# Values of the first four pieces loaded in fp32 by SyncE's queue, with the first steps of a retention and hard-swish kernel put in another order

## The chip, the cores and the metric

The kernel runs on one core of one Trainium2 chip. The metric is the device time of one execution in microseconds (us), lower is better; the median of several runs is given. A core has five engines with a program of their own: TensorE (PE, matrix products), VectorE (DVE), ScalarE (ACT), GpSimd (POOL) and SyncE (SP). Transfers are issued by an engine and carried out by 16 DMA engines. In this kernel POOL issues the loads that change fp32 to fp16 on the way (the profile's queue q0, "software_dynamic"), SP issues plain transfers and transposes (queue q1, "hardware_dynamic").

## What is computed

```python
def _attn_ref(q, k, v):                       # 8 batches, 8 heads, 576 positions, 64 wide
    scores = scale * np.matmul(q, k.transpose(0, 1, 3, 2))
    gamma = 1.0 - 2.0 ** (-5.0 - np.arange(H))
    Dmat = np.where(rel >= 0, gamma[:, None, None] ** rel, 0.0)   # rel = row - column
    return np.matmul(scores * Dmat[None], v)

def _moe_ref(x, w_in, w_out):                 # 4608 tokens, 512 wide, 2048 hidden
    h = x @ w_in
    g = h * np.clip(h + 3.0, 0.0, 6.0) / 6.0
    return g @ w_out
```

The first part is attention with a decay in place of the softmax, so it can be worked off in pieces of 128 positions with a state carried from piece to piece. Its output, 4608 tokens of 512, goes through a two-layer network with a hard swish between the layers.

## The kernel before

**Tiling.** The sequences are cut into pieces of 128 positions of one batch, all 8 heads at once (`pieces`, lines 55 to 61). The first four pieces, 0 to 3, are the first 128 positions of batches 0 to 3; pieces 4 to 7 the next 128 positions of the same batches, and so on. Four pieces make a block of 512 tokens (`xt`), and a block is the unit of the network: `w_in` (G1, lines 438 and 461, 16 chunks `fc` of 128 hidden units), the activation (445 on ACT, 446 on DVE), `w_out` (G2, line 488, or the seven-product form at line 547 from the second block on).

**One piece.** Its keys are turned by PE (`k_by_pe`, line 296) and copied by ACT into the tile `qk`; its queries are turned and scaled by PE (`q_by_pe`, line 304; for pieces 0 to 3, which `EARLY = 4` names, against the tile `d2`, line 315) and copied by ACT (line 320). Then come the scores (`scores`, line 346, eight matmuls into one tile `sc`; for piece 3 `scores_two`, line 656, into two banks), the causal mask on DVE (line 350, or 664 for piece 3, with half of it first copied to `raw` by ACT, line 660), the scaled values `vs` on DVE (`scale_v`, line 288), the output `o` by PE (line 378), and its copy into `xt` by ACT (line 261, for piece 3 half by DVE). `update_mm` (line 402) forms the product of keys and values `u`, `update_state` (line 416) scales it by `gc` into the state `ts` on DVE. `spread_state` copies `ts` later into a block-diagonal tile that the pieces of the next round read.

**Order.** The order on each engine is written out by hand (`manual_schedule`). Every engine works its own list in order; a wait at one instruction holds all behind it on that engine. The stretch that the change touches is the start, up to the first full-width G1 matmul (line 438). PE's order there, with `warm` standing for matmuls on zeros of 512 columns: 8 warm; keys 0; 1 warm; queries 0; 2 warm; scores 0; keys 1; 2 warm; queries 1; 3 warm; scores 1; output 0; `u` 0; keys 2; 2 warm; queries 2; output 1; `u` 1; 1 warm; keys 3; scores 2; queries 3; 3 warm; scores 3; output 2; G1 chunks 0 and 1 for the first 256 tokens (line 461); output 3; `u` of 2 and 3; G1 chunks 0 and 1 for the other 256 tokens; then G1 chunks 2 to 15 at full width (line 438).

**Loads.** POOL's list of loads, in order: queries 0; keys 1, queries 1, values 1; keys 2, queries 2; keys 3, queries 3; values 2; 256 columns of `w_in`; values 3; the rest of `w_in` in five loads; half of `w_out`; piece 4; the other half of `w_out`; and so on. All of them change fp32 to fp16 on the way. SP's list begins with two plain fp32 loads of 256 KB, keys 0 and values 0 (`whole`, line 138). ACT casts keys 0 to fp16 (line 192); values 0 go into `scale_v` as fp32.

**Constants.** DVE makes the identity, `d2` (line 183), `dq` (line 188, used from piece 4 on), eight small fills of `lgc` and four fills of the block-diagonal tiles (line 208) before the first mask; ACT makes `gc` (lines 200 and 201) before it copies the turned keys of piece 0 (line 302).

Of the kernel before, what the change touches and what calls it, by code (L numbers as in the profile page):

```python
# [10 lines left out]
FP32 = mybir.dt.float32  # L11
FP16 = mybir.dt.float16
# [5 lines left out]
def kernel(  # L18
# [78 lines left out]
    def by_twos(b, s0):  # L97

        return q[b, :, s0:s0 + P, :].rearrange("h (g t) d -> g h (t d)", t=2)

    def q2_tile(c):

        tag, bufs = (("part1", 1), ("part5", 1), ("part6", 1), ("osb2", 3))[c]
        return work.tile([HALF, H, 2 * D], FP16, tag=tag, bufs=bufs, name=f"q2_{c}")

    def load(c, parts="kqv"):
        if c not in loaded:
            kn = nat.tile([P, H, D], FP16, tag="kn", bufs=NBUF, name=f"kn_{c}")
            qv = nat.tile([P, 2, H, D], FP16, tag="qv", bufs=NBUF, name=f"qv_{c}")
            loaded[c] = {"kn": kn, "qv": qv, "q16": qv[:, 0]}  # L110
            if c < EARLY:
                loaded[c]["q2"] = q2_tile(c)
        to = {"k": (loaded[c]["kn"], k), "q": (loaded[c]["qv"][:, 0], q),
              "v": (loaded[c]["qv"][:, 1], v)}
        for dst, src in (to[part] for part in parts):
            for p0, b, s0, n in pieces[c][3]:
                if src is q and c < EARLY:
                    nc.gpsimd.dma_start(loaded[c]["q2"], by_twos(b, s0))
                    continue
                nc.gpsimd.dma_start(dst[p0:p0 + n],  # L120
                                    src[b, :, s0:s0 + n, :].rearrange("h s d -> s h d"))

# [5 lines left out]
    def load_wout(c0, c1):  # L128
# [6 lines left out]
    wide = const.tile([P, P + 1], FP32)  # L135
    nc.gpsimd.iota(wide, pattern=[[1, P + 1]], base=-1, channel_multiplier=-1,
                   allow_small_or_imprecise_dtypes=True)
    def whole(src, c):

        x = work.tile([P, DM], FP32, tag="osb", bufs=4, name=f"whole_{src.tensor.name}_{c}")  # L140
        x = x.rearrange("s (h d) -> s h d", h=H)
        nc.sync.dma_start(x, src[0, :, c * P:c * P + P, :].rearrange("h s d -> s h d"))
        return x

    k0, v0 = whole(k, 0), whole(v, 0)
    loaded[0] = {"kn": nat.tile([P, H, D], FP16, tag="kn", bufs=NBUF, name="kn_0"),
                 "q2": q2_tile(0), "v": v0}
    nc.gpsimd.dma_start(loaded[0]["q2"], by_twos(0, 0))
    zeros = const.tile([P, MBLK], FP16)
    nc.vector.memset(zeros, 0.0)  # L150
    cb = const.tile([P, 2], FP32)
# [10 lines left out]
    for t in range(2):  # L162
# [21 lines left out]
        out=d2, in0=ident16[0:HALF, None, 0:HALF].to_broadcast([HALF, 2 * H, HALF]),  # L184
        in1=g2q.rearrange("g t h -> g (t h)")[:, :, None].to_broadcast([HALF, 2 * H, HALF]),
        op=ALU.mult)
    dq = const.tile([P, H, P], FP16)
    nc.vector.tensor_tensor(out=dq, in0=ident16[:, None, :].to_broadcast([P, H, P]),
                            in1=gq[:, :, None].to_broadcast([P, H, P]), op=ALU.mult)
    gqv = const.tile([P, 2, H, D], FP16)  # L190
    nc.scalar.copy(gqv[:, 1], gv[:, :, None].to_broadcast([P, H, D]))
    nc.scalar.copy(loaded[0]["kn"], k0)
    lgc = const.tile([P, NPAIR], FP32)
    for p in range(NPAIR):
        nc.vector.memset(lgc[0:HALF, p:p + 1], lng[2 * p])
# [1 line left out]


    gc = const.tile([P, 2, NPAIR], FP32)
    nc.scalar.activation(gc[:, 0], lgc, ACTF.Exp, scale=float(P))  # L200
    nc.scalar.activation(gc[:, 1], lgc, ACTF.Exp, scale=float(HALF))

    def fill_gq():
        nc.scalar.copy(gqv[:, 0], gq[:, :, None].to_broadcast([P, H, D]))
# [1 line left out]
    spare = [const.tile([P, NPAIR, P], FP16, name=f"tbd{i}") for i in range(GROUP)]  # L206
    for bd in spare:
        nc.vector.memset(bd, 0.0)

    warmed = [0]  # L210

    def warm(n, cols):

        if n == 0:
            return
        w = psum.tile([P, MBLK], FP32, tag="ph", bufs=4, name=f"warm_{warmed[0]}")
        warmed[0] += 1
        for _ in range(n):
            nc.tensor.matmul(w[:, 0:cols], zeros[:, 0:P], zeros[:, 0:cols],
                             start=True, stop=True)  # L220

    warm(8, MBLK)

    mask_rest = const.tile([P, P], FP16)

# [56 lines left out]
    def scale_v(c, parts=1):  # L282
        vs = work.tile([P, 2, H, D], FP16, tag="vs", bufs=6, name=f"vs_{c}")
        st.setdefault(c, {})["vs"] = vs[:, 1]
        v16 = loaded[c]["v"] if "v" in loaded[c] else loaded[c]["qv"][:, 1]
        for i in range(parts):
            r = slice(i * H // parts, (i + 1) * H // parts)
            nc.vector.tensor_tensor(out=vs[:, 1, r], in0=v16[:, r], in1=gqv[:, 1, r],
                                    op=ALU.mult)
# [14 lines left out]
    def q_by_pe(c, tag="ph"):  # L304
        qk = qk_of(c)
        pq = psum.tile([P, NPAIR, P], FP32, tag=tag, bufs=4 if tag == "ph" else 1,
                       name=f"trq_{c}")
        if c < EARLY:
            q2 = loaded[c]["q2"]
            pq = pq.rearrange("x p (t g) -> x p t g", t=2)  # L310
            for p in range(NPAIR):
                for t in range(2):
                    for h2 in range(2):
                        h = 2 * p + h2
                        nc.tensor.matmul(pq[h2 * HALF:h2 * HALF + HALF, p, t],
                                         q2[:, h, t * D:t * D + D], d2[:, t * H + h],
                                         start=(p == 0 and t == 0),
                                         stop=(p == NPAIR - 1 and t == 1),
                                         skip_group_check=True)
            nc.scalar.copy(qk[:, 0].rearrange("x p (g t) -> x p t g", t=2), pq)  # L320
            return
        q16 = loaded[c]["q16"]
        for p in range(NPAIR):
            for h2 in range(2):
                r = slice(h2 * HALF, h2 * HALF + HALF)
                nc.tensor.matmul(pq[r, p, :], q16[:, 2 * p + h2, :], dq[:, 2 * p + h2, :],
                                 start=(p == 0), stop=(p == NPAIR - 1), skip_group_check=True)
        nc.scalar.copy(qk[:, 0], pq)
# [61 lines left out]
    def update_mm(cs):  # L390

        cs = [c for c in cs if pieces[c][0] != "rest"]
        if not cs:
            return
        u = psum.tile([P, len(cs), NPAIR, D], FP32, tag="tu", name=f"u_{cs[0]}")
        for j, c in enumerate(cs):
            kn, vs = loaded[c]["kn"], st[c]["vs"]
            st[c]["u"] = u[:, j]
            for p in range(NPAIR):
                for h2 in range(2):  # L400
                    r = slice(h2 * HALF, h2 * HALF + HALF)
                    nc.tensor.matmul(u[r, j, p, :], kn[:, 2 * p + h2, :], vs[:, 2 * p + h2, :],  # L402
                                     start=(j == 0 and p == 0),
                                     stop=(j == len(cs) - 1 and p == NPAIR - 1),
                                     skip_group_check=True)

    def update_state(c):
        kind, b, i, _ = pieces[c]
        if kind == "rest":
            return  # L410
        u = st[c]["u"]
        scale = gc_b[1 if i == PER - 1 and b % 2 else 0]
        tag, bufs = ("tf", B) if i == PER - 1 else ("ts", 2 * GROUP)
        ts = work.tile([P, NPAIR, D], FP16, tag=tag, bufs=bufs, name=f"ts_{c}")
        if i == 0:
            nc.vector.tensor_tensor(out=ts, in0=u, in1=scale, op=ALU.mult)
        else:
            ta = work.tile([P, NPAIR, D], FP32, tag="ta", bufs=2, name=f"ta_{c}")
            nc.vector.tensor_tensor(out=ta, in0=u, in1=state_of[b], op=ALU.add)
            nc.vector.tensor_tensor(out=ts, in0=ta, in1=scale, op=ALU.mult)  # L420
        state_of[b] = ts

    def spread_state(c, copy=nc.scalar.copy):

# [196 lines left out]


    WQ = DFF // 4
    load(1)
    load(2, "kq")
    load(3, "kq")
    load(2, "v")
    load_win(0, WQ // 2)
    load(3, "v")
    for f0, f1 in ((1, 2), (2, 3), (3, 4), (4, 6), (6, 8)):  # L630
        load_win(f0 * WQ // 2, f1 * WQ // 2)
    for i in range(4):
# [4 lines left out]
    def output(c, *tags):  # L637
        inter(c, *tags)
        intra(c)

    def masked(c, filled=0):
        warm(filled, MBLK)
        scores(c, 0)
        run_later(9)
# [24 lines left out]
    k_by_pe(0)  # L669
    warm(1, MBLK)  # L670
    q_by_pe(0)
    warm(2, MBLK)
    masked(0)
    scale_v(0)
    scale_v(1)
    k_by_pe(1)
    warm(2, MBLK)
    q_by_pe(1)
    masked(1, 3)
    output(0)  # L680
    update_mm([0])
    update_state(0)
    k_by_pe(2)
    warm(2, MBLK)
    q_by_pe(2)
    output(1)
    update_mm([1])
    update_state(1)
    warm(1, MBLK)
    k_by_pe(3)  # L690
    masked(2)
    q_by_pe(3)
    scale_v(2)
    warm(3, MBLK)
    mask_two = scores_two(3)
    mask_two()
    scale_v(3, 2)
    output(2)
    for c in range(5, 8):
        load(c)  # L700
    next_load = [8]
# [212 lines left out]
    done, last = slice(0, 3 * P), slice(3 * P, MBLK)  # L914
    for fc in range(2):
        g1_columns(0, fc, banks[fc], slice(0, 2 * P))
    output(3, "o", "sc")
    update_mm([2, 3])
    update_state(2)
# [71 lines left out]
```

## Time and profile before

| what | value |
|---|---|
| median of 3 runs | 292.28 us (292.03 to 293.57) |
| the profiled execution, its own time | 292.02 us |
| its span, first to last instruction | 290.2 us |
| busy in the span: PE / DVE / ACT / POOL | 283.2 / 236.5 / 181.5 / 107.0 us |
| mean granted TensorE clock | 0.997 |

Busy time by stretch of the span (us):

| stretch | PE | DVE | ACT | POOL | moved, GB/s |
|---|---|---|---|---|---|
| 0 to 7 | 5.15 | 5.38 | 4.31 | 6.09 | 140 |
| 7 to 10 | 2.64 | 2.14 | 1.69 | 3.00 | 161 |
| 10 to 15 | 4.87 | 3.82 | 3.72 | 5.00 | 178 |
| 15 to 20 | 4.96 | 4.06 | 3.49 | 3.85 | 202 |
| 20 to 25 | 5.00 | 4.41 | 3.95 | 1.35 | 206 |
| 25 to 30 | 5.00 | 4.88 | 4.34 | 1.66 | 185 |
| 30 to 40 | 10.00 | 4.13 | 2.20 | 6.35 | 181 |

PE's busy time before the full-width G1 contains the matmuls on zeros, which compute nothing: a busy PE is no progress there. Progress is read from the chain of waits, and from when the first full-width G1 matmul begins.

### The profile page before, as it was taken

The page shows a single profiled execution, that of the slowest core. Times are in us where ns is not written, and L with a number is a line of the kernel's source. Part 1 is how long each engine was busy: PE and PEld are TensorE (multiplying, and loading weights), DVE is VectorE, ACT ScalarE, POOL GpSimd, SP SyncE. Part 2 cuts the span into 40 slices and gives each one's busy share as a digit, 9 for nine tenths or more (in the row PEclk, how much of TensorE's full clock was granted, in tenths as well). Part 3 has the DMA queues.
Part 4 walks back from the last instruction along what each step waited for, and adds up shares of the span by engine and source line. Part 5 has one row for each costly group of instructions (what it writes and reads, how often), then busy time and mean ns, then how long its engine had stood idle before and what let it go on. Part 6 is the DMA issues. An engine that isn't in the chain of part 4 may idle for free.

```text
span 290.2 us, 6739 instructions
## 1 busy us (share of the span) xinstructions
PE 283.2 (98%) x2702; PEld 185.3 (64%) x2702; DVE 236.5 (81%) x409; ACT 181.5 (63%) x312; POOL 107.0 (37%) x134
## 2 busy tenths in 40 slices
PE   7999999999999999999999999999999999999993
PEld 2554455548854885478547864787468746874582
DVE  7789559899979986998699869995999599818951
ACT  6678336785578567834785668665876586437711
POOL 8953678610870077007700770067455000000000
PEclk9999999999999999999999999999999999999998
DMA  9999999999999399919992999199999550021014
GB/s 141 171 203 198 192 156 216 172 150 107 105 215 158 70 97 218 150 36 100 212 152 50 88 215 169 23 90 201 174 73 97 114 127 0 2 84 64 1 38 110
DMA packets 151808, 35.84 MB, mean 123 GB/s; under 512 B 141536, under 2 KB 147680, under 8 KB 151776
## 3 DMA queue, kind: packets, MB, share of 16 engines
q0 software_dynamic: 113664, 18.10, 88.3%
q1 hardware_dynamic: 37808, 17.05, 29.1%
q8 instruction: 21, 0.34, 0.5%
q10 hardware_dynamic: 304, 0.26, 0.3%
q14 instruction: 11, 0.09, 0.1%
HBM read 36.70 MB, written 9.44 MB: 159 GB/s over the span
## 4 chain that ended last, share of the span: by engine, by line
PE 94%; DMA 2%; ACT 1%; DVE 1%; ACTq 0%; issue 0%; POOL 0%; POOLq 0%
PE ph L438 41%; PE b L547 19%; PE c L547 10%; PE pout L488 5%; PE a L547 5%; PE o L378 4%; PE sc L346 2%; PE o L267 2%; PE ph L461 2%; DMA q<-in_q_dram 2%; PE u L402 1%; PE sc L766 1%; PE trk L301 1%; ACT qk L320 1%; ACTq L478 0%; PE o L273 0%
## 5 line engine op out<-in xcount | busy, mean ns | idle before, releaser
L445 ACT ACTIVATE u<-ph,cb 128x512 f32<-128x512 f32 x144 | 98.5, 689 | 25.4 <-PE ph L438 23.3
L446 DVE SCALAR_TENSOR_TENSOR gt<-u,ph 128x512 f16<-128x512 f32 x144 | 95.8, 685 | 20.9 <-ACT u L445 18.5
L438 PE MATMUL ph<-xt,win 128*128 128x512 f16 x488 | 106.6, 379 | 0.0
L438 PEld LDWEIGHTS <-win 128*128 128x128 f16 x552 | 54.0, 98 | 63.2
L120 POOL DMA_DIRECT2D kn<-in_k_dram x39 | 33.4, 860 | 91.1 <-PE u L402 77.0
L547 PEld LDWEIGHTS <-s 128*128 128x128 f16 x512 | 49.4, 98 | 6.6 <-DVE s L521 0.2
L547 PEld LDWEIGHTS <-gt 128*128 128x128 f16 x384 | 36.3, 98 | 7.4 <-DVE gt L446 1.1
L120 POOL DMA_DIRECT2D qv<-in_v_dram x39 | 34.0, 880 | 4.1 <-DMA kn<-in_k_dram 1.9
L120 POOL DMA_DIRECT2D qv<-in_q_dram x36 | 30.9, 864 | 6.5 <-DMA wout<-in_moe_w_out_dram 3.4
L547 PE MATMUL b<-tw,s 128*128 128x256 f16 x256 | 30.6, 273 | 0.0
L350 DVE TENSOR_TENSOR at<-sc,mask_wide 128x1024 f16<-128x1024 f32 x19 | 23.2, 1223 | 8.4 <-PE sc L346 8.4
L261 ACT CAST xt<-o 128x512 f16<-128x512 f32 (+1 forms) x32 | 17.2, 576 | 19.2 <-PE o L378 17.2
L521 DVE TENSOR_TENSOR s<-gt 128x512 f16<-128x512 f16 (+1 forms) x37 | 22.7, 614 | 0.1
L557 ACT COPY part<-b 128x512 f32<-128x512 f32 x14 | 8.2, 586 | 20.1 <-PE b L547 20.1
L336 DVE TENSOR_TENSOR vs<-qv,gqv 128x1024 f16<-128x1024 f16 x28 | 19.2, 686 | 0.0
L547 PE MATMUL b<-wout,gt 128*128 128x256 f16 x128 | 15.6, 273 | 0.0
L547 PE MATMUL b<-tw,gt 128*128 128x256 f16 x128 | 15.3, 273 | 0.0
L547 PE MATMUL c<-tw,s 128*128 128x256 f16 x128 | 15.3, 273 | 0.0
L547 PE MATMUL a<-wout,gt 128*128 128x256 f16 x128 | 15.3, 273 | 0.0
L547 PE MATMUL c<-wout,s 128*128 128x256 f16 x128 | 15.3, 273 | 0.0
L772 ACT CAST raw<-sc 128x512 f16<-128x512 f32 x28 | 15.1, 592 | 0.0
L488 PE MATMUL pout<-wout,gt 128*128 128x512 f16 x64 | 14.8, 379 | 0.0
(96 smaller groups left out, 276.1 us busy)
## 6 DMA issues: line engine op xcount, KB each, us to landing
kn<-in_k_dram POOLq DMA_DIRECT2D x31, 128.0 KB, 5.8
qv<-in_v_dram POOLq DMA_DIRECT2D x31, 128.0 KB, 6.1
qv<-in_q_dram POOLq DMA_DIRECT2D x28, 128.0 KB, 6.5
out_dram<-olo SPq DMA_DIRECT2D x7, 512.0 KB, 4.4
out_dram<-ohi SPq DMA_DIRECT2D x7, 512.0 KB, 4.8
wout<-in_moe_w_out_dram POOLq DMA_DIRECT2D x4, 512.0 KB, 14.6
win<-in_moe_w_in_dram POOLq DMA_DIRECT2D x4, 256.0 KB, 6.4
win<-in_moe_w_in_dram POOLq DMA_DIRECT2D x2, 512.0 KB, 10.0
```

Source lines behind the costliest of these rows:

```text
L120: nc.gpsimd.dma_start(dst[p0:p0 + n], src[b, :, s0:s0 + n, :].rearrange("h s d -> s h d"))
L261: engines[i](xt[:, i * self.n:(i + 1) * self.n, g0:g0 + P], bank)
L336: nc.vector.tensor_tensor(out=vs, in0=loaded[c]["qv"], in1=gqv, op=ALU.mult)
L350: mask = lambda: nc.vector.tensor_tensor(out=at.rearrange("t a b s -> t (a b) s"), in0=sc.rearrange("t a b s -> t (a b) s"), in1=mask_b[pi ...
L378: nc.tensor.matmul(o.pair(p, r), vs[:, 2 * p + h2, :], at[:, h2, p, :], start=(st[c]["first"] and o.begins(p)), stop=(o.ends(p) and not mo ...
L438: nc.tensor.matmul(ph, win16[:, dmc, P * fc:P * fc + P], xt_of(kb)[:, dmc, :], start=(dmc == 0), stop=(dmc == NCC - 1))
L445: nc.scalar.activation(u, ph, ACTF.Relu, bias=cb[:, 0:1], scale=1.0 / 6.0)
L446: nc.vector.scalar_tensor_tensor(out=gts[kb][:, fc, :], in0=u, scalar=1.0, in1=ph, op0=ALU.min, op1=ALU.mult)
L488: nc.tensor.matmul(pout, gt[:, fc, P * mc:P * mc + P], wout16[:, fc, :], start=(fc == 0), stop=(fc == NFC - 1))
L521: nc.vector.tensor_tensor(out=sm[i][:, q], in0=one, in1=other, op=op)
L547: nc.tensor.matmul(my[chain][tt], left[:, k, P * tt:P * tt + P], right[:, k, :], start=(first and (tt == 0 or apart) and k == 0), stop=(k ...
L772: nc.scalar.copy(raw[:, h2], banks[h2])
```

## The change

It touches the start alone. Values 0 to 3 are all loaded by SP as fp32, 256 KB each, into tiles of their own; the first of them goes into the tile `raw` that keys 0 have been cast out of, so its issue waits for that cast, and the three others are issued behind it. POOL no longer loads values 1, 2 and 3, and its loads behind them move up. The tiles `qv` of pieces 0 to 3 are gone. `scale_v` for pieces 1 to 3 reads fp32 in place of fp16.

On PE the matmuls on zeros go from 22 to 16, and the order becomes: 7 warm; keys 0; 1 warm; queries 0; 3 warm; scores 0; keys 1; 2 warm; queries 1; 3 warm; scores 1; keys 2; queries 2; output 0; keys 3; scores 2; queries 3; output 1; `u` of 0 and 1 into one bank; scores 3; G1 chunks 0 and 1 for the first 256 tokens; output 2; output 3; `u` of 2 and 3; G1 chunks 0 and 1 for the other 256; then G1 at full width as before.

The states of pieces 0 and 1 are made by ACT in four multiplications (`first_states`), each over both pieces and one pair of heads, between ACT's copy to `raw` and its copy of output 2; DVE's two multiplications for them go. On DVE `dq` moves behind the fills of the block-diagonal tiles, and values 1 are scaled behind mask 1 instead of ahead of it. ACT makes `gc` after its copies of the turned keys and queries of piece 0 instead of before them. ACT's copy of the queries of pieces 0 to 3 writes in order and reads in strides, where it read in order and wrote in strides.

```diff
     def load(c, parts="kqv"):
-        if c not in loaded:
...
+        if "kn" not in loaded.setdefault(c, {}):
+            loaded[c].update({"kn": nat.tile([P, H, D], FP16, tag="kn", bufs=NBUF, name=f"kn_{c}")})
             if c < EARLY:
                 loaded[c]["q2"] = q2_tile(c)
+            else:
+                qv = nat.tile([P, 2, H, D], FP16, tag="qv", bufs=NBUF, name=f"qv_{c}")
+                loaded[c].update(qv=qv, q16=qv[:, 0])
...
-    def whole(src, c):
+    def whole(src, c, tag="osb", bufs=4):
...
-        nc.sync.dma_start(x, src[0, :, c * P:c * P + P, :].rearrange("h s d -> s h d"))
+        _, b, s0, n = pieces[c][3][0]
+        nc.sync.dma_start(x, src[b, :, s0:s0 + n, :].rearrange("h s d -> s h d"))
         return x
-    k0, v0 = whole(k, 0), whole(v, 0)
+    k0 = whole(k, 0, "raw", 1)
...
     nc.scalar.copy(loaded[0]["kn"], k0)
+    for c in range(EARLY):
+        loaded.setdefault(c, {})["v"] = whole(v, c, *(() if c else ("raw", 1)))
...
-    warm(8, MBLK)
+    warm(7, MBLK)
...
-            nc.scalar.copy(qk[:, 0].rearrange("x p (g t) -> x p t g", t=2), pq)
+            nc.scalar.copy(qk[:, 0].rearrange("x p (g t) -> x p g t", t=2),
+                           pq.rearrange("x p t g -> x p g t"))
...
+    def first_states(cs):
+        ts = work.tile([P, len(cs), NPAIR, D], FP16, tag="ts2", bufs=1, name=f"ts_{cs[0]}")
+        u = st[cs[0]]["u_all"]
+        for p in range(NPAIR):
+            nc.scalar.mul(ts[:, :, p, :], u[:, :, p, :], gc[:, 0, p:p + 1])
+        for j, c in enumerate(cs):
+            state_of[pieces[c][1]] = ts[:, j]
...
-    load(1)
-    load(2, "kq")
-    load(3, "kq")
-    load(2, "v")
+    for c in range(1, EARLY):
+        load(c, "kq")
     load_win(0, WQ // 2)
-    load(3, "v")
...
     q_by_pe(0)
-    warm(2, MBLK)
+    warm(3, MBLK)
     masked(0)
     scale_v(0)
-    scale_v(1)
+    fill_gc()
     k_by_pe(1)
     warm(2, MBLK)
     q_by_pe(1)
     masked(1, 3)
+    scale_v(1)
+    k_by_pe(2)
+    q_by_pe(2)
     output(0)
-    update_mm([0])
-    update_state(0)
-    k_by_pe(2)
-    warm(2, MBLK)
-    q_by_pe(2)
-    output(1)
-    update_mm([1])
-    update_state(1)
-    warm(1, MBLK)
     k_by_pe(3)
     masked(2)
     q_by_pe(3)
+    output(1)
     scale_v(2)
-    warm(3, MBLK)
+    update_mm([0, 1])
     mask_two = scores_two(3)
     mask_two()
     scale_v(3, 2)
-    output(2)
+    first_states([0, 1])
...
     for fc in range(2):
         g1_columns(0, fc, banks[fc], slice(0, 2 * P))
+    output(2)
     output(3, "o", "sc")
     update_mm([2, 3])
```

More of the change, by code (lines that the diff above doesn't have):

```diff
@@ L106, in load @@
     def load(c, parts="kqv"):
-        if c not in loaded:
-            kn = nat.tile([P, H, D], FP16, tag="kn", bufs=NBUF, name=f"kn_{c}")
-            qv = nat.tile([P, 2, H, D], FP16, tag="qv", bufs=NBUF, name=f"qv_{c}")
-            loaded[c] = {"kn": kn, "qv": qv, "q16": qv[:, 0]}
+        if "kn" not in loaded.setdefault(c, {}):
+            loaded[c].update({"kn": nat.tile([P, H, D], FP16, tag="kn", bufs=NBUF, name=f"kn_{c}")})
             if c < EARLY:
                 loaded[c]["q2"] = q2_tile(c)
-        to = {"k": (loaded[c]["kn"], k), "q": (loaded[c]["qv"][:, 0], q),
-              "v": (loaded[c]["qv"][:, 1], v)}
-        for dst, src in (to[part] for part in parts):
+            else:
+                qv = nat.tile([P, 2, H, D], FP16, tag="qv", bufs=NBUF, name=f"qv_{c}")
+                loaded[c].update(qv=qv, q16=qv[:, 0])
+        for part in parts:
+            src = {"k": k, "q": q, "v": v}[part]
             for p0, b, s0, n in pieces[c][3]:
-                if src is q and c < EARLY:
+                if part == "q" and c < EARLY:
                     nc.gpsimd.dma_start(loaded[c]["q2"], by_twos(b, s0))
                     continue
+                dst = loaded[c]["kn"] if part == "k" else loaded[c]["qv"][:, "qv".index(part)]
                 nc.gpsimd.dma_start(dst[p0:p0 + n],
@@ L137 @@
                    allow_small_or_imprecise_dtypes=True)
-    def whole(src, c):
-        x = work.tile([P, DM], FP32, tag="osb", bufs=4, name=f"whole_{src.tensor.name}_{c}")
+    def whole(src, c, tag="osb", bufs=4):
+        x = work.tile([P, DM], FP32, tag=tag, bufs=bufs, name=f"whole_{src.tensor.name}_{c}")
         x = x.rearrange("s (h d) -> s h d", h=H)
-        nc.sync.dma_start(x, src[0, :, c * P:c * P + P, :].rearrange("h s d -> s h d"))
+        _, b, s0, n = pieces[c][3][0]
+        nc.sync.dma_start(x, src[b, :, s0:s0 + n, :].rearrange("h s d -> s h d"))
         return x
-    k0, v0 = whole(k, 0), whole(v, 0)
+    k0 = whole(k, 0, "raw", 1)
     loaded[0] = {"kn": nat.tile([P, H, D], FP16, tag="kn", bufs=NBUF, name="kn_0"),
-                 "q2": q2_tile(0), "v": v0}
-    nc.gpsimd.dma_start(loaded[0]["q2"], by_twos(0, 0))
+                 "q2": q2_tile(0)}
+    load(0, "q")
     zeros = const.tile([P, MBLK], FP16)
@@ L186 @@
         op=ALU.mult)
-    dq = const.tile([P, H, P], FP16)
-    nc.vector.tensor_tensor(out=dq, in0=ident16[:, None, :].to_broadcast([P, H, P]),
-                            in1=gq[:, :, None].to_broadcast([P, H, P]), op=ALU.mult)
     gqv = const.tile([P, 2, H, D], FP16)
@@ L199, with fill_gc @@
     gc = const.tile([P, 2, NPAIR], FP32)
-    nc.scalar.activation(gc[:, 0], lgc, ACTF.Exp, scale=float(P))
-    nc.scalar.activation(gc[:, 1], lgc, ACTF.Exp, scale=float(HALF))
+    def fill_gc():
+        nc.scalar.activation(gc[:, 0], lgc, ACTF.Exp, scale=float(P))
+        nc.scalar.activation(gc[:, 1], lgc, ACTF.Exp, scale=float(HALF))
     def fill_gq():
@@ L208 @@
         nc.vector.memset(bd, 0.0)
+    dq = const.tile([P, H, P], FP16)
+    nc.vector.tensor_tensor(out=dq, in0=ident16[:, None, :].to_broadcast([P, H, P]),
+                            in1=gq[:, :, None].to_broadcast([P, H, P]), op=ALU.mult)
     warmed = [0]
@@ L395, in update_mm @@
         u = psum.tile([P, len(cs), NPAIR, D], FP32, tag="tu", name=f"u_{cs[0]}")
+        st[cs[0]]["u_all"] = u
         for j, c in enumerate(cs):
```

## The prediction, made before the result

> **What bounds the kernel now.** I read the chain of waits first, then its pieces in the first 20 us in order of time, then the timeline, then the DMA queues in short stretches. On the whole span the page says of the chain:
>
> ```profile
> PE 94%; DMA 2%; ACT 1%; DVE 1%; ACTq 0%; issue 0%; POOL 0%; POOLq 0%
> ```
>
> PE sets the end. From the first full-width G1 matmul on, the change alters no instruction, and PE is 100% busy from 20 to 60 us, so what the change is worth is how far that first matmul moves. The chain up to it (start, duration, what):
>
> ```profile
> 1.35 4.76 DMA q<-in_q_dram
> ...
> 6.16 0.46 PE trq L315 x16
> ...
> 13.16 1.23 DVE at L350
> 14.39 0.34 DVE vs L288
> ...
> 16.87 1.04 PE ph L461 x8
> 17.91 2.16 PE ph L438 x10
> ```
>
> Full-width G1 begins at 17.91. Ahead of it stand queries 0, landing at 6.11, then a ladder of PE, ACT and DVE steps; the last rungs are the masks and scalings of pieces 2 and 3 on DVE. Now the rows that I price with (timeline, then one landing of the DMA issues, us after the issue):
>
> ```profile
> 3.90 0.62 ACT L192 CAST kn<-whole_in_k_dram 128x512 f16<-128x512 f32 x1 [0.56 <-DMA whole_in_k_dram<-in_k_dram]
> ...
> 7.03 0.74 POOL L118 DMA_DIRECT2D q<-in_q_dram  x1
> ...
> 7.86 1.23 DVE L350 TENSOR_TENSOR at<-sc,mask_wide 128x1024 f16<-128x1024 f32 x1 [1.00 <-PE sc L346]
> ...
> 15.73 0.49 DVE L288 TENSOR_TENSOR vs<-qv,gqv 128x256 f16<-128x256 f16 x2
> ```
>
> ```profile
> q<-in_q_dram POOLq DMA_DIRECT2D x1, 128.0 KB, 5.4
> ```
>
> Queries 3 land at 7.03 + 5.4 = 12.43, and PE turns them at 13.05, only 0.6 later: the loads are close behind the ladder. Between queries 0 (6.11) and queries 3 seven loads of POOL land, 0.90 us apart. The DMA engines are busy throughout (nines in every slice from 4 us on), so this is a full queue. What a second queue does to it, from the queue rows (packets, MB, share) of 2 to 4, 40 to 44, 45 to 47 and 62 to 64 us in turn:
>
> ```profile
> q1 hardware_dynamic: 1898, 0.48, 108.2%
> ```
>
> ```profile
> q0 software_dynamic: 4842, 0.61, 239.7%
> ```
>
> ```profile
> q0 software_dynamic: 1230, 0.16, 123.5%
> q1 hardware_dynamic: 206, 0.38, 52.3%
> ```
>
> ```profile
> q0 software_dynamic: 1082, 0.14, 104.8%
> q1 hardware_dynamic: 736, 0.17, 69.0%
> ```
>
> SP's fp32 loads of keys 0 and values 0 ran alone at 0.24 MB/us, so 0.26 MB takes 1.05 us. POOL's queue alone makes 4842 / 4 = 1210 packets per us; beside SP's stores 615, beside SP's transposes 541. What SP's queue moves, POOL's queue loses.
>
> **The change part by part.** *Queries 0.* Before, POOL's queue had only 19 packets moved by 4.0 us, 2.6 us after its first issue, while values 0 were still moving. A load that POOL issues at 74.43 into an idle queue has its first packets in the slice at 76.0, 1.6 us after. Without values 0 in front, queries 0 land between 6.11 (nothing gained) and 5.2 (0.9 earlier). I take 5.5, nearer to the idle-queue row.
>
> *Queries 3 without SP's values.* Values 1 leave the queue ahead of them, so six loads stand between: 5.5 + 6 x 0.90 = 10.9.
>
> *SP's four values.* The first waits for the cast of keys 0, which ends at 4.52; the other three stand behind it on SP, at about 0.55 us each by SP's row for values 0, and nothing else waits on SP that early. Keys 0 took 3.1 us from issue to landing, of which 1.05 are their own bytes, and values 0 landed 1.1 after their last packets, so the first packets come 3.1 - 1.05 - 0.9 = 1.2 after the issue: 5.75. By then POOL's queue stands at what would land at 5.75 + 1.1 = 6.85, 1.35 us of work past queries 0, and 5.4 - 1.35 = 4.05 us are left before queries 3. SP's four loads are 4 x 1.05 = 4.2 us of the same engines. If the two halve them, both end together and queries 3 land 4.05 later, at 14.95. The price is not shown for this very pair. Bounds: nothing (SP's loads free beside POOL's); by the stores, 0.98 us of POOL's queue lost for 0.38 MB, so 2.7 for 1.05 MB; by the transposes POOL's queue keeps 0.45 of its rate, so 4.05 / 0.45 = 9.0 us for what is left, 0.9 more than at a half. I take the half: SP's own loads have just these 256 B rows, and the stores too left POOL's queue a half (615 of 1210).
>
> The Trainium skill says the same in "DMA: Bandwidth & Descriptors", section "Issuing engines are not separate DMA queues": whichever engine starts them, transfers run on the same 16 DMA engines and interleave, and starting them on several saves only issue time. By that rule the sum is the one made here, and without it the first rival's; the 615 of 1210 packets agree.
>
> How the engines are shared hardly matters: if SP's values come first, queries 3 are as late; if POOL's loads come first, values 0 land after 11 instead of at 8.7, and DVE, in order, holds mask 1 and all behind it.
>
> *From queries 3 to G1.* Before: 13.05 to 17.91, 4.86 us. After, the same rungs: turn, copy, scores, two masks, scaling, output 3, half copy, 8 matmuls. Scaling from fp32 costs 0.68 (row of values 0, 9.00) for 0.49: +0.19. The copy of queries took 0.74 with strided writes; a plain one of that size takes 0.59; I take 0.65, bounds 0.59 and 0.80: -0.09. ACT's four state products: copies of 512 and 256 columns cost 0.59 and 0.37, so about 0.26 for 128, 1.04 together, between `raw` and the copy of output 2. They run while DVE finishes mask 3 and scales (0.43 + 0.68), which covers them; 0.05, at most 0.3. So 5.0. The 16 G1 matmuls of 256 tokens now stand before output 2, and their `w_in`, right behind queries 3 in the queue, is there in time (1.3 us of queue, while turn, copy and scores take 1.5).
>
> *At no cost:* `dq` behind the fills (same sum, DVE still free at 6.86, a mask not due before 7); six warm matmuls fewer (PE waits for loads there); `gc` later; two state products off DVE (0.41 + 0.43), which DVE would spend waiting for scores 2.
>
> *Sum.* PE takes queries 3 at 15.0 instead of 13.05, +1.95; the path +0.15; G1 at 20.0 instead of 17.91: +2.1 us. Later loads arrive about 1 us later at most, less than G1's own shift, so nothing gives it back or adds. The profiled execution, 290.2 us of span in 292.02, becomes 294.1; the median is 0.26 above it: **294.4 us**.
>
> **The rivals.** *A, faster: SP's loads cost POOL's queue little.* Then DVE sets the pace. It is free at 6.86, where it idled 1.00 us before mask 0; from there 3 x 1.23 + 4 x 0.68 + 0.69 + 0.43 = 7.53 us back to back end scaling 3 at 14.39 instead of 16.22: -1.83, **290.5**. It decides if SP's values delay queries 3 by less than 0.55 us (10.9 to the 11.45 at which they are due). For it: both queues together moved 0.54 MB in 2 us at 45, against 0.31 for POOL's alone. Against it: POOL's packets halved there.
>
> *B, about the same: the stores' price.* Queries 3 land 2.7 late, 13.6: +0.6 on PE, +0.15 on the path: **293.0**. Against it: packets of 256 B move fewer bytes per us than the stores'.
>
> *C, much slower: the transposes' price and a cold PE.* Queries 3 land at 15.85, +0.9 over the main case. PE then waits some 3 us between output 0 and keys 3 with no matmuls on zeros left to fill it. The first eight of those took 3.60 us, 0.43 each; later two take 0.43. If that half rate returns, a few us of matmuls double; I price it at 0.8: **296.1**. "TensorE: Matmul & The Clock Gate" of the Trainium skill, section "What's actually happening", puts the return to half rate after an idle window of about 3.4 us; the trace shows only the half rate at the start.
>
> **Numbers.** What this kernel's measurement can tell from no change is about 0.5%, 1.46 us. Main case 0.43 (own range 293.5 to 295.5), A 0.31, B 0.14, C 0.12. Slower is the main case, less a thin edge, and C: 0.54; same is B and that edge: 0.15; faster A: 0.31. The range takes in A to C, 290.0 to 296.2.
>
> **What would show it.** Queue q0 near 600 packets per us between 6 and 14 us, with q1 beside it: the main case; near 1200: A. Queries 3 landing near 15, not near 11. PE idle before keys 3. Mask 0 starting near 7. Full-width G1 at 20.0; at 16.1 A holds, at 18.6 B. I am wrong if POOL's queue keeps its rate, or if queries 0 land before 5.

## The result and the profile after

The changed kernel takes 301.8 us (median of 6 runs, 301.23 to 304.24) against 292.89 us for the kernel before on the same chip: a ratio of 1.032, with a 95% interval of 1.028 to 1.037. It is slower, as forecast, but by 8.9 us and not by 2.1, and outside the range. The profiled execution took 301.43 us, with a span of 299.4 us (before: 290.2) and a mean granted clock of 0.977.

First the page of the kernel after: the engines' shares in the chain that ended last, and the granted clock in 40 slices of 7.5 us.

```profile
PEclk9956999999999999999999999999999999999999
...
PE 90%; DMA 6%; SPq 2%; ACT 0%; ACTq 0%; DVE 0%; issue 0%
```

PE's share fell from 94 to 90%; DMA and SP's issues now have 8%, where DMA had 2%. Slices 3 and 4 (15 to 30 us) run at half and six tenths of full speed. Where the DMA stands in the chain shows in its pieces in order of time, up to the first full-width G1 (line 455 now; start, duration, what):

```profile
5.45 3.74 SPq L144
...
9.24 14.50 DMA whole_in_v_dram<-in_v_dram
23.74 0.02 issue
23.76 0.44 DVE vs L294
...
24.25 0.76 PE o L385 x6
...
25.43 1.82 PE ph L478 x8
27.25 0.90 PE ph L455 x4
```

Values 3, issued by SP at 9.24, land at 23.74. Everything waits for them: DVE scales them at 23.76, PE forms output 3, the last eight G1 matmuls of 256 tokens, and full-width G1 begins at 27.25. Before, it began at 17.91. That is 9.3 us, and the two spans differ by 9.2: the whole loss lies ahead of this matmul. (In the timeline it begins some 0.2 us earlier than in the chain, at 27.04 here and at 17.75 before; where a run below shows a timeline, it is compared with these.) The scaling of values 3 began at 15.73 before, so 8.0 of it is the late landing; the other 1.3 is that the stretch from the scaling to G1 took 3.49 us instead of 2.18, nearly all of it the clock's: the last eight G1 matmuls of 256 tokens took 1.82 us where they had taken 1.04. The first row below is the wait behind it (waits of the first 28 us: total, times, longest), the next three the stretches 10 to 15, 15 to 20 and 20 to 25 us (busy time of each engine with its instructions, then granted clock, DMA share, GB/s):

```profile
DVE vs L294 <- DMA whole_in_v_dram<-in_v_dram: 8.9, 4, 3.0
```

```profile
10.00:15.00 5.00, 1.55 (x32) 1.13 (x32) 2.49 (x3) 1.66 (x3) 1.56 (x3) 0.86 1.61 188
15.00:20.00 5.00, 4.87 (x67) 3.19 (x65) 1.73 (x3) 3.37 (x8) 2.28 (x3) 0.50 1.35 185
20.00:25.00 5.00, 1.39 (x24) 1.00 (x26) 1.92 (x5) 0.88 (x2) 2.50 (x3) 0.50 1.26 200
```

DVE waited at each of the four scalings. PE was busy 1.55 of 5 us between 10 and 15, and then worked at half rate. Why SP's loads took so long shows in the queue rows of 7 to 9, 15 to 17 and 20 to 22 us in turn (packets, MB, share):

```profile
q0 software_dynamic: 722, 0.11, 73.3%
q1 hardware_dynamic: 862, 0.22, 70.1%
...
q0 software_dynamic: 491, 0.24, 87.6%
q1 hardware_dynamic: 492, 0.13, 47.0%
...
q0 software_dynamic: 376, 0.29, 90.2%
q1 hardware_dynamic: 377, 0.10, 36.0%
```

From about 14 us on, POOL's queue carries `w_in` in packets of 0.24 MB / 491 = 490 bytes and more, and SP's queue moves as many packets as POOL's, one for one. But its packets are of 256 B, so it moves 0.06 MB per us, a quarter of the 0.24 it made alone. At that pace the half megabyte of values 2 and 3 takes 8 us. (The first two rows, from 7 to 9 us, are not one for one: there POOL's queue carries keys and queries in packets of about 150 bytes.)

### The profile page after: what moved, and what is told of

The parts are those of the page before. It is cut to its first block, busy times and chain, and to the rows that moved or that the text cites. A ratio compares the mean times of both kernels' runs of the same rounds, so it can differ in the third digit from the quotient of the medians.

```text
span 299.4 us, 6732 instructions
## 1 busy us (share of the span) xinstructions
PE 286.4 (96%) x2696; PEld 186.8 (62%) x2696; DVE 237.2 (79%) x407; ACT 182.3 (61%) x316; POOL 104.4 (35%) x131
## 4 chain that ended last, share of the span: by engine, by line
PE 90%; DMA 6%; SPq 2%; ACT 0%; ACTq 0%; DVE 0%; issue 0%
PE ph L455 40%; PE b L564 19%; PE c L564 10%; DMA whole_in_v_dram<-in_v_dram 5%; PE pout L505 5%; PE a L564 5%; PE o L385 3%; PE sc L353 2%; PE o L273 2%; PE ph L478 2%; SPq L144 2%; PE u L410 1%; PE sc L775 1%; DMA whole_in_k_dram<-in_k_dram 1%; ACTq L495 0%; PE o L279 0%
## 5 line engine op out<-in xcount | busy, mean ns | idle before, releaser
L121 POOL DMA_DIRECT2D qv<-in_v_dram x36 | 31.2, 876 | 3.7 <-DMA wout<-in_moe_w_out_dram 2.2
L385 PE MATMUL o<-at,vs 128*64 128x128 f16 x288 | 13.1, 230 | 3.7 <-DVE vs L294 3.7
```

Of the source, the lines that this page charges most:

```text
L121: nc.gpsimd.dma_start(dst[p0:p0 + n], src[b, :, s0:s0 + n, :].rearrange("h s d -> s h d"))
L385: nc.tensor.matmul(o.pair(p, r), vs[:, 2 * p + h2, :], at[:, h2, p, :], start=(st[c]["first"] and o.begins(p)), stop=(o.ends(p) and not mo ...
```

## Experiments

"Theory 1" in the expectations is this: the loads of SP are late because POOL's queue takes every second turn with larger packets. "Theory 2" puts a loss into the new order of the engines' work. "Before" in each experiment is the kernel before on the same chip. Where no interval is given, the time is that of one execution; the six of the kernel after spread from 301.23 to 304.24, so these times are good to some 3 us, and the traces carry the argument.

**The order alone.** After's order on every engine, with before's loads.

```diff
-                 "q2": q2_tile(0)}
+                 "q2": q2_tile(0), "v": whole(v, 0)}
...
-    for c in range(EARLY):
-        loaded.setdefault(c, {})["v"] = whole(v, c, *(() if c else ("raw", 1)))
...
-    for c in range(1, EARLY):
-        load(c, "kq")
+    load(1, "kqv")
+    load(2, "kq")
+    load(3, "kq")
+    load(2, "v")
     load_win(0, WQ // 2)
+    load(3, "v")
```

> The changed kernel's order of steps, with the loads as they were: values 0 by SP right behind keys 0, values 1 to 3 by POOL in fp16 at their old places. Theory 1 (SP's values land late because their 256-byte packets take turns, one for one, with ever wider packets of POOL's queue): no value is late, queries 3 land near 12.4, full-width G1 begins between 16.8 and 18.2, time within 1.2 us of before. Theory 2 (the new order with fewer matmuls on zeros is what costs, by PE's waits and a lost clock): G1 begins after 20, at least 3 us slower than before.

Measured: 292.99 us against 292.62, ratio 1.000 (0.998 to 1.002). PE's timeline around output 3:

```profile
16.71 0.41 PE L386 MATMUL o<-at,vs 128*64 128x128 f16 x8 [0.68 <-ACT xt L268]
...
18.37 9.88 PE L456 MATMUL ph<-xt,win 128*128 128x512 f16 x45
```

Full-width G1 begins at 18.37 (17.75 before), a little later than expected: output 3 now waits 0.68 us for ACT's copy of output 2. The new order alone neither costs nor gains.

**The queues alone.** Before's order, with after's loads: `load` and `whole` of the changed kernel, and these lines.

```diff
-    k0, v0 = whole(k, 0), whole(v, 0)
+    k0 = whole(k, 0, "raw", 1)
...
     nc.scalar.copy(loaded[0]["kn"], k0)
+    for c in range(EARLY):
+        loaded.setdefault(c, {})["v"] = whole(v, c, *(() if c else ("raw", 1)))
...
-    load(1)
-    load(2, "kq")
-    load(3, "kq")
-    load(2, "v")
+    for c in range(1, EARLY):
+        load(c, "kq")
     load_win(0, WQ // 2)
-    load(3, "v")
```

> The order of steps of before, with the changed kernel's loads: values 0 to 3 by SP, the first waiting for the cast of keys 0. Theory 1: values 3 land near 23.7 as in the changed kernel, G1 begins between 26 and 28, 8 to 10 us slower than before. Theory 2: the old order and its fillers keep most of the time, less than 3 us slower.

Measured: 301.65 us, 9.0 above before. The chain of this kernel up to G1:

```profile
5.42 4.03 SPq L144
...
9.49 14.61 DMA whole_in_v_dram<-in_v_dram
...
27.61 0.49 PE ph L442 x2
```

These are the same pieces as in the kernel after, up to 0.4 us apart. The change of queues alone brings the whole cost, and the new order alone none.

**Values first.** The same four loads, issued directly behind keys 0 instead of behind its cast, each into a tile of its own.

```diff
     k0 = whole(k, 0, "raw", 1)
+    for c in range(EARLY):
+        loaded.setdefault(c, {})["v"] = whole(v, c)
...
     nc.scalar.copy(loaded[0]["kn"], k0)
-    for c in range(EARLY):
-        loaded.setdefault(c, {})["v"] = whole(v, c, *(() if c else ("raw", 1)))
```

> The changed kernel, with SP's four values issued straight behind keys 0 into tiles of their own, not behind the cast. Theory 1: all 4096 packets take turns with keys and queries alone, before any wide packet, so values 3 land by 12.5; queries 3 land at 14 to 15.5, since the work ahead of them is the same; G1 begins between 18.5 and 20.5, 0.5 to 2.5 us slower than before. Theory 3: values 3 land after 18, 4 us or more slower.

Measured: 294.41 us, 1.8 above before. Values 3 land at 13.63, queries 3 at 14.79, and the chain goes on from there:

```profile
14.83 0.46 PE trq L321 x16
...
17.05 1.04 ACT ts L436 x4
18.09 0.48 ACT xt L267
18.62 0.32 PE o L385 x4
...
20.41 7.77 PE ph L455 x36
```

The bytes, the queue and the order are those of the kernel after; what differs is the moment of issue, some 3 us earlier for the first three loads and 5.6 for the fourth (and values 0 have a tile of their own), and 7 us of the loss are gone. What is left is close to the prediction's main case (queries 3 at 14.95, G1 at 20.0). The chain also runs through ACT's four state products, which the prediction had held to be covered.

**Wider packets of `w_in`.** The kernel after, with `w_in` behind its first 256 columns in two loads of 1024 and 768 columns, so that POOL's packets beside SP's are of some 2 KB.

```diff
-    for f0, f1 in ((1, 2), (2, 3), (3, 4), (4, 6), (6, 8)):
+    for f0, f1 in ((1, 5), (5, 8)):
```

> The changed kernel, with w_in behind its first 256 columns loaded in two transfers of 1024 and 768 columns (packets of 2048 and 1536 bytes in SBUF) instead of five of 256 and 512. Theory 1 (one for one by packets): from about 14 us SP's queue falls from 240 to some 100 packets per us, values 3 land between 27 and 32, G1 begins 4 to 9 us later than in the changed kernel (27.2). Theory 3 (SP's queue slow by itself, or sharing by bytes): values 3 land within 1.5 us of 23.7 and G1 begins within 2 us of 27.2.

Measured: 308.76 us, 16.3 above before. Queue rows of 16 to 18 us, and the chain:

```profile
q0 software_dynamic: 184, 0.35, 93.4%
q1 hardware_dynamic: 186, 0.05, 18.4%
```

```profile
9.53 21.61 DMA whole_in_v_dram<-in_v_dram
```

Again one for one, now 184 to 186; SP's queue is down to 0.025 MB per us and values 3 land at 31.15. SP's loads were not touched: the size of POOL's packets sets their time.

**Narrower packets of `w_in`.** The same the other way: the first 1024 columns in 16 loads of 64 columns, 128 B packets.

```diff
-    load_win(0, WQ // 2)
-    for f0, f1 in ((1, 2), (2, 3), (3, 4), (4, 6), (6, 8)):
+    for f0 in range(0, 2 * WQ, 64):
+        load_win(f0, f0 + 64)
+    for f0, f1 in ((4, 6), (6, 8)):
```

> The changed kernel, with the first 1024 columns of w_in loaded in 16 transfers of 64 columns (packets of 128 bytes in SBUF) instead of four of 256. Theory 1 (one for one by packets): beside narrow packets SP's queue makes 400 to 500 packets per us instead of 240, values 3 land by 18, G1 begins between 19 and 22, 2 to 5 us slower than before. Theory 3 (SP's queue is slow by itself, as its third issue of 3.7 us suggests, or the two queues share by bytes): values 3 still land after 22, 8 us or more slower than before.

Measured: 299.44 us, 6.8 above before. Queue rows of 14 to 16 us, then PE's timeline:

```profile
q0 software_dynamic: 1099, 0.14, 106.2%
q1 hardware_dynamic: 718, 0.18, 68.6%
```

```profile
18.63 1.01 PE L478 MATMUL ph<-xt,win 128*128 128x256 f16 x4 [0.78 <-DMA win<-in_moe_w_in_dram]
...
23.57 4.63 PE L455 MATMUL ph<-xt,win 128*128 128x512 f16 x19
```

SP's queue moves 359 packets per us instead of 245 or so, and values 3 land at 18.34, 5.4 us earlier. The time missed: the narrow loads bring `w_in` late, PE waits for it, at half clock, and G1 begins at 23.57. Beside packets this small the turns were not one for one: POOL's queue made 1.5 packets to SP's one; from 7 to 9 us in the kernel after it made 0.84. So for these loads the rule of equal turns is shown beside packets of 0.5 to 2 KB only.

**Values 2 and 3 by a third queue.** The kernel after, with values 2 and 3 issued by ACT.

```diff
-        nc.sync.dma_start(x, src[b, :, s0:s0 + n, :].rearrange("h s d -> s h d"))
+        queue = nc.scalar if src is v and c > 1 else nc.sync
+        queue.dma_start(x, src[b, :, s0:s0 + n, :].rearrange("h s d -> s h d"))
```

> The changed kernel, with values 2 and 3 issued by ScalarE's queue instead of SyncE's, right behind the cast of keys 0 (two issues of about 0.4 us on ScalarE's list); values 0 and 1 stay with SyncE. Theory 1 (the queues take turns packet for packet, so what is left in SyncE's queue when the w_in loads begin crawls): with a third queue POOL's gets about a third of the turns while both others have work, the four values get two thirds, so all values are through before the wide packets of w_in come: values 3 land by 16 instead of 23.74, queries 3 between 15 and 17.5, and the first full-width G1 matmul begins between 20.5 and 23 instead of 27.25; time 294.5 to 297.5. Rival (fp32 loads of the kind that SyncE issues are slow beside POOL's queue whatever queue they are on, or a total of some 790 packets per us is the limit): values 3 land after 20 and the time stays above 299.

Measured: 297.14 us, 5.1 above before. Queue rows of 10 to 12 us (q10 is ACT's) and the chain:

```profile
q0 software_dynamic: 565, 0.12, 64.8%
q1 hardware_dynamic: 584, 0.15, 54.2%
q10 hardware_dynamic: 469, 0.12, 26.9%
```

```profile
15.62 0.61 PE trk L308 x4
...
23.17 6.04 PE ph L456 x28
```

Three queues, in this stretch about a third of the packets each (35, 36 and 29%). All values are in by 15.49, hardly into the stretch in which POOL's queue carries `w_in`, and queries 3 at 16.31. So the same fp32 loads are not slow by nature; they were slow for what stood opposite. (The two loads are also issued earlier, at 3.65 and 4.14 instead of 5.45 and 9.24, so the run doesn't tell the third queue from the earlier issue.) G1 begins at 23.17, just beyond the bound expected, since PE reaches keys 3 at half clock (trk took 0.61 us, 0.40 at full speed).

**Half-size loads.** In the kernel after, SP's third issue takes 3.74 us, which could itself hold values 2 and 3 back. Here each value load is cut into two of 64 positions.

```diff
-        nc.sync.dma_start(x, src[b, :, s0:s0 + n, :].rearrange("h s d -> s h d"))
+        for i in range(0, n, HALF) if src is v else (0,):
+            j = i + HALF if src is v else n
+            nc.sync.dma_start(x[i:j], src[b, :, s0 + i:s0 + j, :].rearrange("h s d -> s h d"))
```

> The changed kernel, with each of SyncE's four value loads cut into two loads of 64 positions (128 KB each). In the changed kernel the third issue took 3.74 us and the fourth 2.55, and SyncE's queue moved only 25 to 136 packets per us between 11 and 13 us. Theory 1 (turns per packet set the landing; the stall of the issues costs little): values 3 land between 22.5 and 25 and the time is within 1 us of the changed kernel's 301.4. Rival (the stall of the long issues, which holds the next load back, costs about 3 us: 800 packets at 240 per us): with smaller loads the stall moves, no stretch below 150 packets per us is left between 7 and 16 us, and values 3 land at 19 to 21.5; time 297.5 to 299.

Measured: 303.02 us, 10.95 above before. The chain, in which no issue is longer than 1.50 us now:

```profile
7.13 1.50 SPq L146
...
11.56 12.52 DMA whole_in_v_dram<-in_v_dram
...
27.60 1.71 PE ph L457 x4
```

Values 3 land at 24.09, as late as with whole loads, and SP's queue never falls below 200 packets per us from 7 to 16. So values 3 are as late without any stretch in which the stall leaves SP's queue empty. One reserve: queries 3 land at 13.88 and the first `w_in` columns at 15.57 here, 1.9 and 2.4 us earlier than in the kernel after, so SP's queue met the wide packets sooner, and a gain from the shorter stalls may be hidden by that. The time is more above before than expected, but within the spread of the kernel after; the granted clock is 0.50 in the stretch of 25 to 30 us, where the kernel after has 0.78.

**Matmuls on zeros in PE's waits.** The kernel after with 26 more of them, to price the clock by itself.

```diff
     scale_v(1)
+    warm(6, MBLK)
     k_by_pe(2)
+    warm(6, MBLK)
     q_by_pe(2)
     output(0)
+    warm(4, MBLK)
     k_by_pe(3)
...
     output(2)
+    warm(10, MBLK)
     output(3, "o", "sc")
```

> The changed kernel, with 26 more matmuls on zeros where PE waits for loads (6 ahead of keys 2, 6 ahead of queries 2, 4 ahead of keys 3, 10 ahead of output 3). If the lost clock has a price of its own: the granted clock stays at 1.0 to 24 us, values 3 land as before near 23.7, G1 begins at 25.8 to 26.5 instead of 27.2, time 0.7 to 1.5 us below the changed kernel's. If it has none: G1 within 0.3 us of 27.2.

Measured: 299.93 us, 7.4 above before, where the kernel after is 8.9 above. Stretches of 15 to 20 and 20 to 25 us, and the chain:

```profile
15.00:20.00 5.00, 2.38 (x58) 1.80 (x52) 1.99 (x3) 2.79 (x8) 2.31 (x3) 1.00 1.34 182
20.00:25.00 5.00, 4.98 (x44) 2.17 (x41) 1.81 (x6) 0.96 (x2) 1.64 (x3) 0.66 1.28 202
```

```profile
20.24 3.94 PE warm L225 x10
...
25.94 1.08 PE ph L455 x5
```

With the clock at 1.00 up to 20 us, values 3 land nearly as late (23.47 instead of 23.74), and G1 begins at 25.94 instead of 27.25. Of these 1.31 us the earlier landing is 0.27, so 1.0 is the clock's here; the last ten added matmuls, which end at 24.18, take back some 0.2 us of it themselves. With the 1.3 us by which the stretch behind values 3 grew, the lost clock costs 1.0 to 1.3 us of the 8.9.

**One value by SP.** The order alone, with values 0 issued behind the cast of keys 0 instead of right behind keys 0: one load of SP's beside POOL's.

```diff
-                 "q2": q2_tile(0), "v": whole(v, 0)}
+                 "q2": q2_tile(0)}
...
     nc.scalar.copy(loaded[0]["kn"], k0)
+    loaded[0]["v"] = whole(v, 0, "raw", 1)
```

> The changed kernel's order with the old loads, but values 0 by SP behind the cast of keys 0 (values 1 to 3 by POOL). Theory 1: queries 0 land near 4.9 instead of 6.2; values 0 take turns with narrow packets only and land at 9 to 11; queries 3 land within 0.5 us of 12.3, as the same bytes are ahead of them; G1 begins at 17.8 to 19.5. A theory that any SP load beside POOL's costs more than its own bytes would have queries 3 after 13.5 and G1 after 20.

Measured: 294.53 us, 2.0 above before. Compared with the run with the order alone, queries 0 land at 5.31 instead of 6.17, but queries 3 at 13.71 instead of 12.32: 1.4 later, where at most 0.5 was expected. From the one to the other it is 8.40 us instead of 6.15, so a load that takes 1.05 us by itself sets POOL's queue back by 2.25. Queue rows of 7 to 9 us:

```profile
q0 software_dynamic: 957, 0.12, 93.6%
q1 hardware_dynamic: 871, 0.22, 71.8%
```

Together 914 packets per us; POOL's queue alone made 996 there in the run with the order alone. That drop explains a part of it only; the rest is open.

**Looking for a faster version.** Three kernels. In the first, output 2 goes back ahead of G1's first columns in the order alone, to remove its wait of 0.68 us:

```diff
+    output(2)
     first_states([0, 1])
...
-    output(2)
     output(3, "o", "sc")
```

> The changed kernel's order with the old loads, and output 2 put back ahead of G1's first columns. With those loads the changed order began G1 at 18.4, and output 3 waited 0.68 us for ACT's copy of output 2, which holds the PSUM bank. If that place of output 2 is what the new order loses: the wait is gone and G1 begins at 17.3 to 17.8, 0.6 to 1.1 us earlier. If the loads (w_in at 14.6, values 3 at 15.4) set it: within 0.3 us of 18.4.

Measured: 292.9 us against 292.5. The wait is gone, but the clock was granted late in this one execution (0.54 between 7 and 10 us), and the states of 2 and 3 waited 0.40 for ACT; G1 began at 18.62. Inconclusive. The second is the kernel before with values 0 loaded by POOL in fp16, between keys 1 and queries 1, so that nothing stands in front of queries 0:

```diff
-    k0, v0 = whole(k, 0), whole(v, 0)
+    k0 = whole(k, 0)
...
-    load(1)
+    load(1, "k")
+    load(0, "v")
+    load(1, "qv")
```

> The kernel before, with values 0 loaded by POOL in fp16 between keys 1 and queries 1 instead of by SP in front of everything. If SP's fp32 burst is what holds POOL's first load back, and one queue by itself loses nothing to taking turns: queries 0 land at 4.9 to 5.3 instead of 6.1, queries 3 at 11.6 to 12.2 instead of 12.4, G1 begins at 16.9 to 17.5, 0.4 to 1.0 us faster than before. Rival: POOL's first load has that latency anyway; then queries 0 land at 6, values 0 push all behind them back by 0.9 and G1 begins 0.3 to 0.9 us later than before.

Measured: 292.47 us against 292.98, ratio 0.999 (0.997 to 1.000). Queries 0 land at 5.12 instead of 6.11, but queries 3 at 13.10 instead of 12.44, and G1 begins at 18.12 in the timeline, against 17.75: the head start of 1 us is more than used up on the way, since values 0 now stand in POOL's queue ahead of queries 1 and push back all behind them, as the rival had it. The third puts the two together, on the new order with one more matmul on zeros at the start (besides the two edits just shown):

```diff
-    warm(7, MBLK)
+    warm(8, MBLK)
```

> The changed kernel's order, with output 2 back ahead of G1's first columns, eight matmuls on zeros at the start, and all values by POOL in fp16 (values 0 between keys 1 and queries 1). If loads and order each give what the looks so far suggest: G1 begins at 16.3 to 17.3, 0.6 to 1.6 us faster than before. If ACT's state products, which stand ahead of its copy of output 3 and hold the PSUM bank of the next products, take it back: G1 at 17.4 to 18.2, within 0.5 us of before.

Measured: 292.9 us against 292.98, ratio 1.000 (0.998 to 1.002). Queries 3 land at 13.04, G1 begins at 18.23; the G1 of 16.3 to 17.3 is missed, and the second case comes out, at its upper end. No version beats the kernel before by more than can be measured.

## Why the prediction was wrong

**Right: what bounds the kernel, the sign, and the weight of one matmul.** PE sets the end behind full-width G1; G1 moved by 9.3 us and the span by 9.2. POOL's queue does lose what SP's moves, and more (722 packets from 7 to 9 us against 2092 before). But the sign came out right by another path: the sum ran through queries 3, the measured chain runs through values 3. Queries 3 land at 15.76, 0.8 later than the 14.95 of the sum and close to the 15.85 of rival C, and there is some luck in that: queries 0 came 0.6 earlier than the 5.5 of the sum, and the way from them to queries 3 took 10.9 us instead of 9.45.

**Wrong: "How the engines are shared hardly matters".** This is the step that failed, with the words before it, "both end together". The sum shared the engines for just as long as POOL had keys and queries to load, and took SP's values to be through when queries 3 were. They weren't. By the rows of one microsecond each, SP's queue had moved up to 15 us some 2470 of the 4096 packets of its four loads (1 MB in packets of 256 B), where the sum has them all through by then, and behind queries 3 POOL's queue goes straight on with `w_in`. From about 14 us on SP's queue got one packet of 256 B for each of POOL's packets of 0.5 KB and more. Values 2 landed at 19.51 and values 3 at 23.74, 8 us after queries 3. In the kernel before, values 1 to 3 stood in POOL's queue in the order in which they are needed, values 3 ahead of most of `w_in`. The change took this order away, and nothing in the two queues puts what is urgent first. Four runs bear on it: packets of 2 KB opposite made it 7.4 us later, packets of 128 B 5.4 earlier, a third queue for two values brought all in by 15.49, and an earlier issue brought back the main case. The prediction also put the issue of each further load at 0.55 us; the third took 3.74 and the fourth 2.55, which left SP's queue nearly idle from 11 to 13 us (136 and 25 packets per us), but with the loads cut in two, and no such gap, values 3 were as late.

The trace of before already had such a row. The prediction took the price beside SP's transposes, 541 packets per us, from the whole stretch of 62 to 64 us, in the last half microsecond of which SP's queue was running out (106 packets to 433). While both had work, from 62 to 63.5 us, POOL's packets and SP's were nearly equal in number:

```profile
q0 software_dynamic: 649, 0.08, 82.6%
q1 hardware_dynamic: 630, 0.15, 79.4%
```

Beside SP's stores they were not (1230 to 206, the prediction's third row), and no run here shows why.

The Trainium skill says in "DMA: Bandwidth & Descriptors", section "Queues, rings and completion order", that each DMA engine goes round the queues for which it has work, a packet at a time. A packet in the Trainium skill is a bundle, typically of 9 to 17 descriptors; whether the profile's packets are these bundles, no run here shows. If one of the profile's packets is what takes a turn, the counts of 491 and 492 agree, and those of 1230 and 206 don't. Read that way, together with the packet sizes, the section would have pointed to the result; the section cited in the prediction, on issuing engines, tells only that the transfers interleave.

**Wrong: the landing of queries 0.** They land at 4.89, earlier than the lower bound of 5.2 and ahead of the 5 that the prediction had named as a sign of being wrong. It gained nothing, since DVE then waited for values 0 until 11.67. The prediction had named that wait, "DVE, in order, holds mask 1", as what would happen if POOL's loads came first; it happened, and mattered less than values 3.

**Mis-sized: ACT's state products.** Put at 0.05, at most 0.3, as covered by DVE. In the run with values first they are in the chain, and the path from queries 3 to G1 took 20.41 - 14.83 = 5.6 us instead of 5.0. With before's loads output 3 waited 0.68 for ACT's copy of output 2. In the kernel after, the late values hide it.

**Mis-sized, in rival C: the cold PE.** C was right that PE would fall back to half rate, and put it at 0.8; it measured 1.0 to 1.3. "TensorE: Matmul & The Clock Gate" of the Trainium skill, section "What's actually happening", ties the fall to an idle window of about 3.4 us. Here no wait of PE ahead of it was longer than 1.65 us; but PE was busy for only 1.55 of 5 us, and the clock fell.

**Refuted: rivals A and B.** POOL's queue did not keep its rate, and lost more than beside the stores: queries 3 at 15.76, not at 10.9 or 13.6. The remark that `w_in` "is there in time" held nearly: its first columns landed at 17.95 and were used at 18.00.

## What to carry to other kernels

One queue is also an order of priority: loads that are moved to a second queue no longer come before the bulk that used to stand behind them, and while both had work beside `w_in` here, they got their turns by packets, so the queue with the smaller packets got the smaller share of the bytes. Ahead of such a move, list what the other queue carries until the *last* moved load is in, not only until the first load of interest, and price it by packets. If a second queue is wanted, issue its loads before the other queue reaches its wide packets; here an issue 3 us earlier (5.6 for the last load) made a difference of 7 us.

## What the hardware showed that was not expected

- SP's loads and `w_in` shared the engines packet for packet: 491 to 492 beside packets of 0.5 KB, 376 to 377 beside some 0.8 KB, 184 to 186 beside 2 KB; three queues had about a third each in one stretch (565, 584, 469). Beside POOL's narrow packets of some 130 to 150 B the split went either way (1099 to 718, 722 to 862), and beside SP's stores it was 1230 to 206.
- SP's third load of 256 KB took 3.74 us to issue and the fourth 2.55, where the first took 0.38: the third ended at 9.20, about when the first load's packets were through (911 of 1024 up to 9 us, 377 more in the next). Cutting the loads in two spread the stall over the last issues and did not bring values 3 earlier.
- One load of SP's, 1.05 us by itself, set POOL's queue back by 2.25 us.
- PE lost its clock without any long wait: short pieces of work, 1.55 us in 5, between waits of 0.9 to 1.65 us were not enough to keep it.
